# Splitting one weight load and two weight casts into halves, with a newly written order of all steps, in a fused linear-attention and feed-forward kernel

## The chip, the cores and the metric

The kernel runs on one core of one Trainium2 chip. The metric is the device time of one execution in microseconds, the median of several runs. Five engines work side by side, each through its own instruction queue: TensorE (PE in the profile; PEld is its weight load), VectorE (DVE), ScalarE (ACT), GpSimd (POOL) and SyncE (SP), which here issues transfers. An engine takes its instructions strictly in the order in which the program issues them to it, so an instruction that waits holds up all behind it.

## The reference

The first half is a gated linear attention for 4 batches of 8 heads, 768 tokens and a head size of 48: per head a 48x48 state is decayed by a gate and updated for each token, and each output is the query times the state. The second half treats the 3072 tokens with 384 features through a feed-forward layer with h*cos(h) as its nonlinearity.

```python
f = 1.0 / (1.0 + np.exp(-f_logit))
for t in range(S):
    state = f[:, :, t, :, None] * state + np.einsum('bhd,bhe->bhde', k[:, :, t], v[:, :, t])
    y[:, :, t] = np.einsum('bhd,bhde->bhe', q[:, :, t], state)
...
h = x @ w_in            # 3072x384 by 384x2048
g = h * np.cos(h)
return (g @ w_out).astype(np.float32)
```

## The kernel before

**Tiling.** The attention runs over 12 pairs (`pair`, lines 315 to 579), each 256 tokens of one batch for all 8 heads; three pairs make a batch and hand the state on. A pair works in chunk form: gates and their running sums, scaled copies of q and k, scores inside a chunk, sums of k and v over a chunk, and the product with the carried state. The feed-forward layer runs in 13 units (`moe`, lines 589 to 646): units 0 and 1 have 128 tokens each (both halves of pair 0), every later unit m has the 256 tokens of pair m-1. All products are in bf16 with sums in f32. w_in (384x2048) and w_out (2048x384) are loaded as f32 in four quarters each into staging tiles and cast to bf16 (`weights`, lines 275 to 289).

**Steps.** `describe` builds a graph of 930 named steps, each with the engines it may run on and the values it reads and writes. The names used below, with n the pair or m the unit:

- loads on SP (lines 298 to 313): f, k, q, v with n; those of pairs 0 and 1 except v come in two halves by heads (f0.0, f0.1). w0.i and w1.i load quarter i of w_in and w_out (line 286).
- casts of weights: wc0.i and wc1.i (line 288; line 198 in the profile, since `copy` records it).
- ACT: ex, ln, fx, fy make gates from f; eb, ei are exponentials of the running sums; co is the cosine (line 617); xe, ot, vb, vt, sm are copies and casts that several engines may do.
- DVE and POOL: qa, ka (lines 340 to 355) and qm, km (line 408) scale q and k; ad, sd, st, am and g (line 584, the gated product) are elementwise products and sums. zf (line 268), zsp, zqk and zvt are a product of zeros on TensorE that nothing reads, and the clearing of buffers.
- PE: cum (running sums), tq and tk (transpositions; pairs 5 to 11 do them by a DMA), sc (scores), ps (sums over a chunk, line 492), y and yi (outputs, line 545), h (w_in, line 612: `h{m}.{j}{s}` is half s of block j) and o (w_out, line 634: `o{t}.{s}` is quarter s of the sum for token block t).

A unit of 128 tokens reads a whole quarter of w_in in one step h (four blocks of columns, 128 each); a unit of 256 tokens reads half a quarter (two blocks):

```python
G.step(f"h{m}.{j}{s}", ("PE",), first, reads=[xw, w_in_v[(j * F + s * F // 2) // 4]],
       writes=[ph], sums=True)
```

**What sets the order.** Nothing at run time: the text `ORDER` (lines 39 to 118) lists all steps in one sequence, with a letter for the engine (T for PE, S for ACT, V for DVE, G for POOL, Y for SP) and the buffer slots for what the step writes. `emit` (lines 660 to 682) issues them in that order, so each engine's queue is the sequence of its letter, and waits follow from what a step reads, writes and from who had its slot before. The staging tiles of the weights share the slots of g; PSUM is eight banks of 512 (T0 to T7). The 44 zf stand early among the PE steps: TensorE multiplies zeros while the first real inputs come in.

**SP's order before**, as far as it matters: the halves of pairs 0 and 1 with v0, v1 and f2, then w0.0, w0.1, w0.3, w0.2, q2, w1.0, w1.1, k2, w1.2, v2, f3, w1.3, f4, v3, k3, k4, q4, f6, q3.

Of the kernel before, what the change touches and what calls it, by code (L numbers as in the profile page):

```python
# [44 lines left out]
cum1.1:T0 ei1.1:S1 k1.1:Y1 ka0.1:V km0.1:V vb0:G0 vt0.1:G1 qkt0.0:V0 zf23:T3 tk0.1:T k1.0:Y fx1.1:S
v1:Y1 eb1.1:S1 zf24:T3 sc0.0:T4 am0.01:V0 qkt0.1:S1 am0.00:V q1.0:Y f2:Y0 zf25:T3 ps0.0:T0,2 qa1.1:V
vt0.3:S w0.0:Y0 ka1.1:G ex1.0:S ps0.1:T sc0.1:T6 am0.10:V1 sd0.0:V0 am0.11:V st0.1:V km1.1:G1 vt0.2:S
ln1.0:S zf26:T1 zf27:T1 zf28:T1 zf29:T1 zf30:T5 zf31:T5 zf32:T5 cum1.0:T3 vt0.0:S fx1.0:S eb1.0:S
ei1.0:S sm0.0:S0 ka1.0:V vb1:S0 y0.0:T0 zf33:T5 tk1.1:T1 y0.1:T3 w0.1:Y1 vt1.3:S1 vt1.2:S yi0.1:T
xe0.0:S0 km1.0:V qm1.1:V qa1.0:V qm1.0:G zf34:T5 zf35:T5 ps1.1:T6,7 ps1.0:T sd0.1:V0 st1.0:V tq1.1:T  # L50
sd1.0:V1 tk1.0:T4 qkt1.1:V0 w0.3:Y2 w0.2:Y3 sm1.0:G0 zf36:T2 zf37:T2 tq1.0:T zf38:T2 sc1.1:T0 sm0.1:G1
q2:Y0 w1.0:Y4 qkt1.0:V1 ex2:S ln2:S0 xe0.1:S wc0.0:S zf39:T2 sc1.0:T4 zf40:T2 zf41:T2 yi1:T6,2
ad2:G2 zf42:T3 zf43:T3 cum2:T3 vt1.1:G am1.1:V0 vt1.0:G fy2:S h0.00:T0 wc0.1:G am1.0:V1 w1.1:Y0
fx2:S eb2:S0 y1:T st1.1:V xe1.0:V1 ei2:S1 xe1.1:S k2:Y1 sd1.1:V1 h1.00:T4 h2.00:T2 w1.2:Y1
h0.01:T h1.01:T h2.11:T6 wc0.3:G zqk.0:G co0.0:S0 wc0.2:G g0.0:V2 h2.01:T h2.10:T co1.0:S1 g1.0:V
h0.11:T0 co2.1:S2 h0.10:T qa2:G h1.11:T4 h1.10:T co2.0:S0 qm2.1:G0 g2.1:V3 wc1.0:G qm2.0:G co0.1:S1
v2:Y1 co1.1:S2 g2.0:V h2.20:T6 h2.21:T co2.2:S0 h2.31:T2 h2.30:T co2.3:S3 sm1.1:S0 wc1.1:G g0.1:V
g1.1:V g2.2:V o3.0:T0 o0.0:T1 o1.0:T4 tq2.1:T5 o3.1:T tq2.0:T6 o1.1:T f3:Y1 ka2:G km2.1:G
tk2.1:T w1.3:Y4 f4:Y0 v3:Y0 zsp.1:G g2.3:V km2.0:V wc1.2:S ex3:S ln3:S0 fx3:S zqk.2:G
tk2.0:T k3:Y0 vb2:G0 o3.2:T qkt2.1:V0 sc2.1:T2 vt2.1:G0 wc1.3:S vt2.3:G ps2.1:T5 ps2.0:T k4:Y1  # L60
o1.2:T qkt2.0:V1 st2.0:V o0.1:T sc2.0:T6 vt2.0:G q4:Y0 sd2.0:V0 o0.2:T am2.1:V0 sm2.0:G1 yi2:T5,2
ex4:S ln4:S1 vt2.2:G fx4:S ad3:G1 fy4:S ad4:G2 am2.0:V1 y2:T xe2.1:V0 xe2.0:V cum3:T3
o3.3:T o0.3:T ot3:V0 ot0:V1 vb3:G0 o1.3:T h3.20:T6 cum4:T2 eb3:S0 ot1:V2 f6:Y2 ei3:S0
ka3:V km3.0:V0 h3.01:T0 ei4:S1 eb4:S1 h3.00:T h3.21:T km3.1:V ps3.0:T2,3 ps3.1:T ka4:G h3.10:T4
sd3.0:V0 st3.1:V h3.11:T sd3.1:V1 qa4:G h3.31:T2 h3.30:T co3.2:S0 g3.2:V0 o4.2:T6 km4.0:G1 q3:Y1
qm4.0:G qm4.1:G q5:Y2 co3.0:S1 o2.3:T7 f5:Y0 v4:Y0 q6:Y0 sm3.1:S0 co3.1:S2 co3.3:S0 out3:Y
out0:Y g3.0:V tk4.0:T0 g3.1:V km4.1:G fy3:S g3.3:V o4.0:T tk3.0:T1 tq4.1:T4 tq4.0:T qkt4.0:V0
o4.1:T qa3:G vt3.1:G0 tk4.1:T o4.3:T tk3.1:T0 qkt4.1:V1 ex6:S ex5:S ln6:S0 ln5:S1 ot4:S3
qm3.1:V sc4.0:T2 sc4.1:T4 am4.0:V0 o2.2:T tq3.1:T o2.0:T qm3.0:G tq3.0:T o2.1:T f7:Y1 v6:Y1
k6:Y0 k5:Y1 vb4:G1 am4.1:V1 vt4.0:S1 v5:Y0 fx5:S ot2:S0 ad5:G1 o5.0:T2 vt3.3:G qkt3.0:V2  # L70
vt4.3:G ps4.0:T1,3 ps4.1:T sc3.0:T4 qkt3.1:V3 sc3.1:T6 ad6:G2 cum5:T0 o5.2:T vt4.1:S vt4.2:S st4.0:V
sm3.0:G1 vt3.2:G fy6:S fx6:S vt3.0:G o5.3:T sd4.0:V2 cum6:T1 eb5:S0 sm4.0:S2 ei5:S0 am3.0:V2
am3.1:V3 zvt.2:V qa6:G y4:T4,5 yi4:T fy5:S ex7:S eb6:S2 yi3:T0 y3:T6 xe4.1:V0 xe4.0:V
# [116 lines left out]
def describe(nc, cpool, ppool, q, k, v, f_logit, moe_w_in, moe_w_out, out):  # L190
# [72 lines left out]

    if ZEROS:
        for i in range(ZEROS):
            dump = Val(p1)
            dump.bank = i if i < 8 else None
            G.step(f"zf{i}", ("PE",), lambda e, dump=dump: nc.tensor.matmul(  # L268
                dump.ap, lhsT=zero[:, 0:128], rhs=zero, start=True, stop=True), writes=[dump])
# [488 lines left out]
```

## Time and profile before

| what | value |
|---|---|
| median of 3 runs | 178.31 us (178.24 to 178.71) |
| profiled execution | 179.66 us, of which the span from first to last instruction is 177.4 |
| PE busy | 170.8 us (96%), 2470 products |
| DVE, ACT, POOL busy | 136.0, 137.7, 100.1 us |
| clock granted to TensorE | 1.00 throughout |
| read and written in HBM | 25.17 and 4.72 MB |

How to read it: a row of the timeline has start, duration, engine, line, operation, output and inputs, a count, and in brackets how long the engine stood idle before it and what ended that. A row of a transfer is its issue on SP; its landing comes some microseconds later, and the list of transfers gives the time from issue to landing. In the chain of waits a row has start, duration, and the work or wait that the chain went through.

### The profile page before, as it was taken

The numbers are of one execution on the slowest core, as the hardware profiler recorded it, in microseconds if no ns is written. First come the engines' busy times: TensorE is split into PE (matmuls) and PEld (weight loads), VectorE is DVE, ScalarE is ACT, GpSimd is POOL, SyncE is SP. The second block draws the span as 40 slices with busy tenths as digits, with TensorE's granted clock in tenths as the row PEclk, the third lists the DMA queues.
The fourth block names the chain that finished last, engine by engine and source line by source line (L and its number), as shares of the span: only waits on it lengthen the run. The fifth ranks groups of instructions, "written<-read, shape, count | busy, mean of one in ns | idle before, by whom it ended". The sixth has DMA issues, their size and how long they took to land.

```text
span 177.4 us, 5843 instructions
## 1 busy us (share of the span) xinstructions
PE 170.8 (96%) x2470; PEld 124.8 (70%) x2470; DVE 136.0 (77%) x196; ACT 137.7 (78%) x205; POOL 100.1 (56%) x128
## 2 busy tenths in 40 slices
...
DMA  5999999989999975999999999997280030010035
GB/s 127 276 261 306 353 352 351 305 229 280 256 258 286 285 185 134 285 171 235 247 260 279 211 227 232 199 155 163 48 193 2 0 137 4 0 44 4 0 113 198
DMA packets 72281, 33.92 MB, mean 191 GB/s; under 512 B 65344, under 2 KB 70720, under 8 KB 72256
## 3 DMA queue, kind: packets, MB, share of 16 engines
q1 hardware_dynamic: 72256, 33.56, 79.5%
q8 instruction: 19, 0.31, 0.8%
...
HBM read 25.17 MB, written 4.72 MB: 168 GB/s over the span
## 4 chain that ended last, share of the span: by engine, by line
PE 75%; DMA 11%; ACT 3%; DVE 3%; SPq 2%; POOL 2%; issue 1%; DVEq 0%; POOLq 0%
PE ps L634 33%; PE ps L612 28%; DMA g<-in_moe_w_in_dram 5%; DMA v<-in_v_dram 5%; PE ps L545 4%; PE ps L462 3%; SPq L286 2%; PE ps L492 2%; PE ps L268 2%; POOL w_in_bf L198 2%; DMA f<-in_f_logit_dram 2%; PE ps L439 1%; DVE am L474 1%; PE ps L378 1%; DVE qk L408 1%
## 5 line engine op out<-in xcount | busy, mean ns | idle before, releaser
L584 DVE TENSOR_TENSOR g<-ps,co 128x1024 bf16<-128x1024 f32 x48 | 60.1, 1309 | 19.2 <-ACT co L617 16.0
L634 PE MATMUL ps<-w_out_bf,g 128*128 128x384 bf16 (+1 forms) x400 | 69.2, 320 | 0.8 <-ACT w_out_bf L198 0.8
L612 PE MATMUL ps<-x,w_in_bf 128*128 128x256 bf16 (+1 forms) x624 | 66.6, 264 | 0.5 <-POOL w_in_bf L198 0.4
L617 ACT ACTIVATE co<-ps,halfpi 128x1024 bf16<-128x1024 f32 x48 | 51.7, 1113 | 18.2 <-PE ps L612 16.3
L612 PEld LDWEIGHTS <-w_in_bf 128*128 128x128 bf16 x624 | 56.5, 98 | 8.4 <-issue 0.6
L634 PEld LDWEIGHTS <-g 128*128 128x128 bf16 x400 | 37.1, 98 | 21.0 <-issue 1.0
L474 DVE TENSOR_TENSOR am<-ps,pmask 128x1024 bf16<-128x1024 f32 x22 | 26.0, 1216 | 1.5 <-PE ps L462 1.4
L408 POOL TENSOR_TENSOR qk<-q,b 128x384 bf16<-128x384 f32 x18 | 17.8, 1003 | 3.4 <-DVE q L342 2.2
L408 POOL TENSOR_TENSOR qk<-k,bi 128x384 bf16<-128x384 f32 x16 | 16.3, 1027 | 4.8 <-issue 2.0
L198 POOL COPY vt<-vb 64x384 bf16<-64x384 bf16 x31 | 15.3, 503 | 1.4
L268 PE MATMUL ps<-zero 128*128 128x512 bf16 x44 | 13.9, 426 | 1.2 <-DVE zero L204 1.2
L198 ACT COPY ot<-ps 128x384 f32<-128x384 f32 (+1 forms) x13 | 5.9, 450 | 8.9 <-PE ps L634 7.2
L198 POOL CAST vb<-v 128x768 bf16<-128x768 f32 x9 | 7.7, 861 | 8.3 <-DMA v<-in_v_dram 8.3
L333 ACT ACTIVATE f<-f 128x768 f32<-128x768 f32 (+1 forms) x14 | 10.3, 751 | 2.5 <-DMA f<-in_f_logit_dram 2.4
L198 DVE CAST x<-ps 128x384 bf16<-128x384 f32 x16 | 8.4, 550 | 4.5 <-PE ps L545 4.4
L519 POOL TENSOR_TENSOR sz<-sd,half 128x384 bf16<-128x384 bf16 x10 | 8.2, 826 | 5.8 <-DVE sd L509 5.5
L367 POOL TENSOR_TENSOR sp<-ls 128x384 bf16<-128x384 f32 x10 | 10.0, 1001 | 2.6 <-ACT ls L337 2.3
L345 POOL TENSOR_TENSOR q<-f,q 128x384 f32<-128x384 f32 x9 | 9.3, 1037 | 1.0 <-DMA q<-in_q_dram 0.4
L355 POOL TENSOR_TENSOR k<-k,f 128x384 f32<-128x384 f32 (+1 forms) x7 | 6.8, 973 | 4.1 <-DMA k<-in_k_dram 2.0
L198 DVE COPY ot<-ps 128x384 f32<-128x384 f32 (+1 forms) x13 | 6.7, 519 | 3.2 <-PE ps L634 3.0
L462 PE MATMUL ps<-qkt 48*64 48x128 bf16 (+1 forms) x304 | 8.9, 219 | 0.1
L198 ACT COPY vt<-vb 64x384 bf16<-64x384 bf16 x17 | 8.6, 508 | 0.3
...
## 6 DMA issues: line engine op xcount, KB each, us to landing
v<-in_v_dram SPq DMA_DIRECT2D x12, 384.0 KB, 5.8
...
f<-in_f_logit_dram SPq DMA_DIRECT2D x10, 384.0 KB, 6.1
q<-in_q_dram SPq DMA_DIRECT2D x10, 384.0 KB, 5.8
k<-in_k_dram SPq DMA_DIRECT2D x10, 384.0 KB, 6.8
g<-in_moe_w_in_dram SPq DMA_DIRECT2D x4, 768.0 KB, 8.5
g<-in_moe_w_out_dram SPq DMA_DIRECT2D x4, 768.0 KB, 10.7
...
```

The lines of the kernel that those rows point to most:

```text
L198: (nc.scalar.copy if e == "ACT" else eng(e).tensor_copy)(out=o, in_=i)
L268: G.step(f"zf{i}", ("PE",), lambda e, dump=dump: nc.tensor.matmul(dump.ap, lhsT=zero[:, 0:128], rhs=zero, start=True, stop=True), writes=[ ...
L333: nc.scalar.activation(out=flat(t.ap), in_=flat(t.ap), func=AF.Exp, scale=-1.0)
L345: eng(e).tensor_mul(out=w.ap[:, :, 0, :], in0=t.ap[:, :, 1, :], in1=w.ap[:, :, 0, :])
L367: G.step(f"ad{n}", ("POOL",), lambda e: eng(e).tensor_add(out=sp.ap[:, 0, :, 0:D], in0=soft.ap[:, :, 0, :], in1=soft.ap[:, :, 1, :]), read ...
L408: G.step(f"{nm}{n}.{u}", ("POOL", "DVE"), lambda e, u=u, j=j, src=src, dec=dec: eng(e).tensor_mul(out=qkp[u][j].ap[:, :, :, 0:D], in0=swap ...
L462: nc.tensor.matmul(o[t, r, 2 * a + g, :].rearrange("p (e n) -> p e n", e=2), lhsT=w, rhs=qkv(u)[s, 0, a, g, :, :], start=(a == 0 and g == ...
L474: G.step(f"am{n}.{u}", ("DVE",), lambda e, u=u, sc=sc: nc.vector.tensor_mul(out=am[u].ap.rearrange("p r b n -> p (r b) n"), in0=sc.ap.rear ...
L584: nc.vector.tensor_mul(out=o.rearrange("p b (n e) -> p b e n", e=2), in0=ph.ap.rearrange("p (b e n) -> p b e n", e=2, n=64), in1=co.ap.rea ...
L612: nc.tensor.matmul(ph.ap[:, i * T:(i + 1) * T].rearrange("p (g t) -> p g t", t=C), lhsT=w_in_bf[:, kk, f0:f0 + 128], rhs=xa[:, :, kk, :], ...
L617: G.step(f"co{m}.{j}", ("ACT",), lambda e, ph=ph, co=co: nc.scalar.activation(out=co.ap, in_=ph.ap, func=AF.Sin, bias=halfpi), reads=[ph], ...
L634: nc.tensor.matmul(po.ap[:, 0:c1 - c0], lhsT=gap[:, j, i * C:(i + 1) * C], rhs=w_out_bf[:, j, c0:c1], start=(po.first and j == 4 * s), sto ...
```

## The change

Three things change; the amount of real work doesn't.

1. **Halves of w_in.** Quarter 0 is loaded by two transfers (w0.0a, w0.0b, 256 columns each), and quarters 0 and 1 are cast by two steps each (wc0.0a, wc0.0b, wc0.1a, wc0.1b), which DVE may do as well. Steps h of units with 256 tokens then wait for the half they read; those with 128 tokens still read the quarter.
2. **46 zeros** in place of 44, each of the same 512 columns (a width of its own for each can now be given).
3. **A new `ORDER`** of 935 steps, from a planner that also knows where TensorE's instruction blocks end. 88 steps change their engine: vt 21, xe and ot 11 each, sm 8, qm 8, ka 6, and others; out23.0 is issued by ACT in place of SP. PE's order differs in the first third above all: o2.0 to o2.3 now come before ps3, and h3.00 and h3.01 after it.

SP's new order after the halves of pairs 0 and 1, f2, v0 and v1 (the same fifteen loads, with f2 moved ahead of v0): w0.1, w0.0b, w0.0a, w0.3, w0.2, k2, w1.0, q2, w1.1, v2, w1.3, f3, f4, w1.2, f6, v3, k4, k3, q4, q3. ACT's queue has vb1, wc0.1a, sm0.1, vt1.2, xe0.1, wc0.0b in that order; POOL's has wc0.1b, vt1.1, wc0.0a, vt1.3, sm1.0, wc0.3, wc0.2, ka2, km2.1, wc1.0, qa2, qm2.0, km2.0, qm2.1.

```diff
+CUT_LOAD = (0,)
+CUT_CAST = (0, 1)
+SC8 = 1
...
-ZEROS = 44
+ZEROS = (512,) * 46
...
+    w_in_h = [[v.part(lambda a, z=z: a[:, :, 256 * z:256 * z + 256]) for z in range(2)] for v in w_in_v]
...
+        parts = w_in_h[i] if part == 0 and i in CUT_CAST else [dst]
+        n = len(parts)
+        stages = [stage.part(None) for _ in parts] if n > 1 else [stage]
+        if part == 0 and i in CUT_LOAD:
+            for z, st in enumerate(stages):
+                c = slice(256 * z, 256 * z + 256)
+                G.step(f"w{part}.{i}{'ab'[z]}", ("SP",), lambda e, c=c: eng(e).dma_start(
+                    out=view()[:, :, c], in_=src[:, :, c]), writes=[st])
+        else:
+            G.step(f"w{part}.{i}", ("SP",), lambda e: eng(e).dma_start(out=view(), in_=src), writes=[stage])
+        for z, (st, d) in enumerate(zip(stages, parts)):
+            c = slice(w // n * z, w // n * z + w // n)
+            G.step(f"wc{part}.{i}{'ab'[z] if n > 1 else ''}", ("POOL", "ACT", "DVE") if n > 1 else ("POOL", "ACT"),
+                   lambda e, c=c, d=d: copy(e, d.ap, view()[:, :, c]), reads=[st], writes=[d])
...
-                G.step(f"h{m}.{j}{s}", ("PE",), first, reads=[xw, w_in_v[(j * F + s * F // 2) // 4]],
+                G.step(f"h{m}.{j}{s}", ("PE",), first, reads=[xw, w_in_h[j][s] if T == 2 * C and j in CUT_CAST else w_in_v[(j * F + s * F // 2) // 4]],
```

The part of the new order around the first products with w_in, on all engines:

```diff
+zf44:T6 ps1.0:T vt1.1:G tq1.0:T2 tk1.0:T wc0.0a:G vt1.3:G st1.0:V w1.1:Y0 qkt1.0:V0 h0.01:T6
+sd1.0:V1 xe0.1:S h1.01:T4 wc0.0b:S fx2:S v2:Y1 vt1.0:S sm1.0:G1 sc1.0:T0 wc0.3:G am1.0:V1 st1.1:V
+sd1.1:V0 wc0.2:G h1.00:T h0.00:T yi1:T0,1 y1:T co1.0:S0 zf45:T2 h1.11:T2 xe1.1:V1 xe1.0:S co0.0:S1
```

More of the change, by code (lines that the diff above doesn't have):

```diff
@@ L45 @@
[L45 to L73, printed above, removed]
@@ L113 @@
[L113 to L117 removed]
+zqk.2:V f0.1:Y0 f0.0:Y ex0.0:S zqk.0:G zsp.2:G ex0.1:S ln0.1:S2 ln0.0:S q0.1:Y0 fx0.1:S qa0.1:V
@@ new lines @@
+qkt0.0:V1 w0.1:Y0 am0.10:V0 am0.11:V zf26:T2 zf27:T2 zf28:T2 zf29:T2 sc0.0:T6 am0.01:V1 w0.0b:Y1 ad2:G2
+w0.0a:Y w0.3:Y2 w0.2:Y3 vt0.3:S0 fx1.0:S eb1.1:S1 zf30:T0 zf31:T0 zf32:T0 ps0.0:T2,0 ps0.1:T cum2:T4
+k2:Y0 qa1.1:V ka1.1:V w1.0:Y4 am0.00:V eb2:S2 vt0.0:S ei1.0:S zf33:T5 zf34:T5 zf35:T5 zf36:T5
+zf37:T1 zf38:T1 y0.0:T5 qm1.1:G0 sd0.0:V0 st0.1:V vt0.2:G qa1.0:V km1.1:V sm0.0:G0 eb1.0:S vt0.1:S
+zf39:T6 zf40:T6 zf41:T6 y0.1:T1 ei2:S1 xe0.0:S0 ka1.0:G tq1.1:T3 tk1.1:T vb1:S0 q2:Y0 sd0.1:V1
+qkt1.1:V2 wc0.1a:S zf42:T6 zf43:T6 yi0.1:T sc1.1:T4 ps1.1:T0,3 sm0.1:S0 km1.0:V vt1.2:S0 qm1.0:V am1.1:V0
@@ new lines @@
+wc0.1b:G zf44:T6 ps1.0:T vt1.1:G tq1.0:T2 tk1.0:T wc0.0a:G vt1.3:G st1.0:V w1.1:Y0 qkt1.0:V0 h0.01:T6
+sd1.0:V1 xe0.1:S h1.01:T4 wc0.0b:S fx2:S v2:Y1 vt1.0:S sm1.0:G1 sc1.0:T0 wc0.3:G am1.0:V1 st1.1:V
+sd1.1:V0 wc0.2:G h1.00:T h0.00:T yi1:T0,1 y1:T co1.0:S0 zf45:T2 h1.11:T2 xe1.1:V1 xe1.0:S co0.0:S1
+h2.01:T0 h2.00:T g1.0:V2 h1.10:T fy2:S w1.3:Y1 ka2:G km2.1:G0 wc1.0:G qa2:G f3:Y1 co2.0:S0
+sm1.1:S0 qm2.0:G km2.0:G g0.0:V f4:Y0 co1.1:S1 h2.31:T4 h0.10:T6 h2.30:T qm2.1:G g2.0:V3 h0.11:T
+co2.3:S0 g1.1:V w1.2:Y4 co0.1:S2 h2.11:T0 h2.10:T h2.21:T2 h2.20:T g2.3:V o0.0:T4 o1.0:T5 f6:Y2
@@ new lines @@
+co2.1:S1 g0.1:V g2.1:V v3:Y0 tk2.0:T6 tq2.0:T k4:Y0 k3:Y1 q4:Y0 tq2.1:T7 tk2.1:T qkt2.0:V0
+vb2:G0 vt2.3:G0 wc1.1:S co2.2:S0 o2.0:T0 o1.1:T qkt2.1:S1 g2.2:V sc2.1:T6 ps2.0:T1 ps2.1:T wc1.3:G
+vt2.1:G st2.0:V sd2.0:V1 sm2.0:V1 vt2.2:G ex3:S sc2.0:T2 am2.0:V0 ln3:S0 fx3:S ad3:G0 am2.1:V1
+vt2.0:G o2.1:T o3.0:T1 o0.1:T o3.3:T o3.1:T ex4:S o0.3:T yi2:T2,3 fy3:S y2:T ln4:S0
+cum3:T6 o2.3:T fy4:S wc1.2:G o3.2:T o2.2:T ad4:G0 cum4:T7 o0.2:T vb3:G0 eb3:S0 fx4:S
+ex6:S ln6:S0 fx6:S vt3.3:G0 q3:Y1 xe2.1:V0 xe2.0:V ot2:V0 ot3:V1 ka4:G ot0:V2 eb4:S1
@@ new lines @@
+ei4:S0 h3.20:T2 o1.2:T ei3:S1 h3.21:T v4:Y0 ka3:V km3.1:V0 k5:Y2 km3.0:V h3.10:T0 o1.3:T
+ps3.1:T4,6 qa4:V ps3.0:T sd3.0:V0 km4.1:G2 km4.0:G co3.2:S0 h3.11:T f5:Y0 q6:Y2 out0:Y qm4.1:G
+ot1:S3 qa3:G h3.01:T4 h3.00:T fy6:S g3.2:V0 h3.30:T2 h3.31:T co3.1:S1 qm4.0:G g3.1:V f7:Y1
+co3.0:S0 vt3.0:S tq4.1:T7 o4.1:T0 qm3.0:G co3.3:S1 tk4.1:T g3.0:V v5:Y1 out3:Y vt3.1:G o4.2:T
+tk3.0:T1 st3.1:V g3.3:V tk4.0:T4 o4.0:T sd3.1:V1 tq4.0:T qkt4.0:V0 qkt4.1:S1 tq3.0:T o4.3:T vb4:S1
+qm3.1:G vt4.0:G2 ad6:G0 ps4.1:T2,3 ps4.0:T q5:Y0 k7:Y0 k6:Y1 qkt3.0:V2 st4.0:V sd4.0:V2 ex5:S
@@ L118 @@
+o22.3:T o20.0:T ot22.0:S1 o23.3b:T0 ot22.1:S out22.0:Y out22.1:Y g11.2:V o21.2:T o20.2:T ot20:S2 o18.1:T
+ot18:S1 o21.0:T out20:Y out18:Y ot21:V3 out21:Y o23.2b:T o23.0b:T o23.1b:T ot23.1:S out23.1:Y
 """
```

124 lines of the change are left out of this document (60 added, 64 removed).

## The prediction

> **What bounds the kernel now.** I read the page first, then busy time by stage, then the timeline of single engines in the stages where TensorE loses time, then the transfers.
>
> ```profile
> span 177.4 us, 5843 instructions
> PE 170.8 (96%) x2470; PEld 124.8 (70%) x2470; DVE 136.0 (77%) x196; ACT 137.7 (78%) x205; POOL 100.1 (56%) x128
> DMA  5999999989999975999999999997280030010035
> ```
>
> TensorE is busy 96% of the span, and the transfers (third row, slices of 4.4 us) are full for the first third. The table by stage has span, then busy time of PE, PEld, DVE, ACT and POOL, clock, DMA share and GB/s.
>
> ```profile
> 1.00:21.30 20.30, 19.53 (x269) 10.31 (x269) 16.08 (x48) 16.70 (x36) 8.56 (x15) 1.00 1.08 273
> 21.30:33.10 11.80, 11.38 (x176) 10.49 (x177) 7.69 (x9) 10.66 (x13) 9.27 (x9) 1.00 1.09 352
> 33.10:49.50 16.40, 15.22 (x204) 9.81 (x202) 13.81 (x18) 13.72 (x20) 12.19 (x16) 1.00 1.04 258
> 49.50:174.30 124.80, 124.69 (x1823) 94.19 (x1823) 98.31 (x124) 96.08 (x138) 69.71 (x85) 1.00 0.72 157
> ```
>
> From 49.5 us to the last product TensorE idles 0.1 us in 124.8. So the end is fixed by two numbers: when TensorE enters this gapless stretch, and how much work it has left then. Only the stages before can be won. They lose 1.18 us in 33.10:49.50 and 0.42 us in the stage ahead; the first stage is partly filled with products of zeros, so its busy time hides waiting.
>
> ```profile
> 27.86 5.46 PE L612 MATMUL ps<-x,w_in_bf 128*128 128x128 bf16 x72 [0.39 <-POOL w_in_bf L198]
> 38.71 0.81 PE L634 MATMUL ps<-w_out_bf,g 128*128 128x384 bf16 x4 [0.83 <-ACT w_out_bf L198]
> 49.57 0.31 PE L492 MATMUL ps<-vb,qk 64*64 64x48 bf16 x16 [0.17 <-DVE qk L408]
> ```
>
> All three waits end with a chain from a load: a quarter of w_in, a quarter of w_out, and (third row, step ps3.1) the k tile of pair 3. The rows of a chain below show how.
>
> **The zeros and the tail.**
>
> ```profile
> 5.83 2.53 PE L268 MATMUL ps<-zero 128*128 128x512 bf16 x11
> 167.10 7.19 PE ps L634 x56
> 174.31 0.32 ACT ot L198
> 50.54 0.37 SPq L300 DMA_DIRECT2D f<-in_f_logit_dram  x1
> ```
>
> Eleven zeros span 2.53 us with a last one of 0.38, so one takes (2.53 - 0.38) / 10 = 0.215 us, and two more 0.43 us. I cost them at nothing: they stand before h1.11, where TensorE will wait for weights anyway (next part). If that cover were gone they would cost 0.43 us. The tail stays: after the last product ot23.1 takes 0.32 us on ACT and its store follows. The one store that moves is out23.0, from SP's queue to ACT's. No row shows a transfer issued by ACT; an issue takes 0.37 us on SP (third row), so it costs at most that on ACT ahead of ot23.1, and gains at most that on SP ahead of out23.1: -0.4 to +0.4. I take 0, since both queues have some microseconds between out23.0 and the last step.
>
> **The first products with w_in.**
>
> ```profile
> 12.33 1.44 SPq L286
> g<-in_moe_w_in_dram SPq DMA_DIRECT2D x1, 768.0 KB, 7.2
> 24.26 1.47 POOL L198 CAST w_in_bf<-g 128x1536 bf16<-128x1536 f32 x1 [0.80 <-DMA g<-in_moe_w_in_dram]
> 26.38 1.47 POOL L198 CAST w_in_bf<-g 128x1536 bf16<-128x1536 f32 x1 [0.18 <-DMA g<-in_moe_w_in_dram]
> 15.52 0.82 ACT L198 CAST vb<-v 128x768 bf16<-128x768 f32 x1
> 14.83 0.79 ACT L517 ACTIVATE sz<-sd,mine 128x192 bf16<-128x192 bf16 x2
> 11.69 0.51 ACT L198 COPY vt<-vb 64x384 bf16<-64x384 bf16 x1
> 17.32 0.47 ACT L198 CAST x<-ps 128x384 bf16<-128x384 f32 x1
> ```
>
> The first quarter of w_in is issued at 12.33 us and lands 7.2 us later, at 19.5. In both plans the same fifteen loads stand ahead of the w_in quarters, so in the new plan quarter 1, now first, lands at 19.5 and both halves of quarter 0 by 21.9. A half cast moves 128x768, like vb: 0.82 us in place of 1.47. That splits a wait: the first half could be cast 1.1 us sooner. But units 0 and 1 (128 tokens) still read the whole quarter; only unit 2 reads halves, and it comes later in both plans. So the halves bring nothing on TensorE's path. Splitting the load into rows of 1 KB costs between 0 (rows of 1.5 and 2 KB move alike) and 0.7 us (the difference from twice a 384 KB tile at the pace below, 2.9 us, to 2.2); I take 0, the nearer rows.
>
> The half cast wc0.1a puts a wait into ACT's queue: ACT stands until 19.5 us for quarter 1, and sm0.1, vt1.2 and xe0.1 queue behind. h1.01 needs xe0.1: 19.5 + 0.82 + 0.79 + 0.51 + 0.47 = 22.1 us, and I put TensorE there about 0.5 us earlier. This is hidden by the next wait; without that it would cost the 0.5. Quarters 3 and 2 land where they land now, since the same bytes are ahead: POOL's casts end at 24.26 + 1.47 = 25.7 and 26.38 + 1.47 = 27.85 us. h1.10 reads quarter 2, so it can't start before 27.87, just as h0.11 today (27.86). Up to the first product with w_out both plans have done the same set (but for the two zeros). Today that product, o3.0, starts at 33.15; in the new plan nine steps h of 0.66 us stand from h1.10 to o0.0, which so comes at 27.87 + 5.94 = 33.8. TensorE is 0.65 us behind here.
>
> The Trainium skill, in "DMA: Bandwidth & Descriptors", section "Rules for kernel authors", says that splitting a transfer into two partition halves isn't worth it because both use the same 16 engines in turn. Here the cut is by columns; no run shown has it, and by that rule the term would be 0 too, with no gain from the earlier half.
>
> **The second pair of loads: POOL's queue.**
>
> ```profile
> 31.14 1.46 POOL L198 CAST w_out_bf<-g 128x1536 bf16<-128x1536 f32 x1 [1.16 <-DMA g<-in_moe_w_out_dram]
> 28.98 1.01 POOL L408 TENSOR_TENSOR qk<-q,b 128x384 bf16<-128x384 f32 x1
> 8.36 0.22 PE ps L439 x4
> 39.45 0.40 PE L462 MATMUL ps<-qkt 48*128 48x128 bf16 x8
> 40.14 1.48 PE L634 MATMUL ps<-w_out_bf,g 128*128 128x384 bf16 x8
> 42.63 0.52 PE L545 MATMUL ps<-qkt,sz 128*32 128x128 bf16 x24
> 44.16 2.11 PE L634 MATMUL ps<-w_out_bf,g 128*128 128x384 bf16 x12
> ```
>
> Today q2 lands ahead of w_out's first quarter, and POOL has qa2 and one qm2 done when that quarter lands at 31.1. The new SP order is k2, w1.0, q2: w1.0 again at about 31.1, for the same bytes are ahead, and q2 1.45 us later (the pace is worked out below). POOL's order is ka2, km2.1, wc1.0, qa2, qm2.0, km2.0, qm2.1: 31.14 + 1.46 + 4 x 1.01 = 36.65 us. The transposition tq2.1 waits for that; TensorE would reach it at 33.8 + 1.3 (o0.0, o1.0) + 0.45 (two transpositions of 0.22) = 35.55. So it loses 1.1 us there, about what this whole stage loses today (1.18). From tq2.1 to ps3.0 the plan has 14 steps o and 3 steps h (9.1 + 2.0 by the prices below), and scores, sums, transpositions and two cum for 3.2 (today 0.69 from 39.45 to 40.14 and 1.5 from 42.63 to 44.16; the other scores, cum4 and the transpositions make up the rest): 14.3 us, so ps3.0 at 50.95.
>
> **The k tile of pair 3.** This is the term that decides.
>
> ```profile
> 38.70 2.77 SPq L300 DMA_DIRECT2D k<-in_k_dram  x1
> k<-in_k_dram SPq DMA_DIRECT2D x1, 384.0 KB, 7.7
> 46.12 1.57 SPq L300 DMA_DIRECT2D q<-in_q_dram  x1
> q<-in_q_dram SPq DMA_DIRECT2D x1, 384.0 KB, 6.1
> 46.79 0.79 DVE L355 TENSOR_TENSOR k<-k,f 128x384 f32<-128x384 f32 x1
> 47.69 1.83 DVE L408 TENSOR_TENSOR qk<-k,bi 128x384 bf16<-128x384 f32 x2
> ```
>
> Today k3 is issued at 38.70 and lands 7.7 us later at 46.4; four tiles on, q3 lands at 46.12 + 6.1 = 52.2. So the full queue passes a 384 KB tile each (52.2 - 46.4) / 4 = 1.45 us. The new SP order puts everything ahead of k3 that is ahead of it today, and f6 and k4 as well: 46.4 + 2 x 1.45 = 49.3 us. Behind it stands the same chain, all on DVE: ka3, km3.1, km3.0, and the product. Today it takes from 46.79 to 49.57, 2.78 us. In the new plan: 49.35 + 2.78 = 52.1 us for ps3.0, later than the 50.95 at which TensorE would be there. ps3.0 is 2.55 us later than ps3.1 today.
>
> What is left then:
>
> ```profile
> 91.33 10.48 PE ps L612 x96
> 76.59 3.90 PE ps L634 x24
> ```
>
> Six products with w_in (a step h) take 0.655 us, four with w_out (a step o) 0.65. At ps3.0 the new plan has done h3.10 and o2.0 to o2.3, which today come after ps3.1, and still owes h3.00 and h3.01, which come before: 0.655 + 4 x 0.65 - 2 x 0.655 = 1.95 us less to do. 2.55 - 1.95 = +0.6 us.
>
> **The gapless stretch.** Steps, engines and shapes are the same; 88 steps change engine, mostly vt, xe, ot, ka in both directions. I cost it at the same 0.1 us of idle time. What covers it is slack of DVE (98.3 of 124.8) and ACT (96.1); POOL has 69.7.
>
> **Sum.** Against the profiled execution: last product from 174.3 to 174.9, span 178.0 in place of 177.4. That execution took 179.66 us, 2.3 over its span and 1.35 over the median of the runs shown (178.31). The difference carries over: 178.31 + 0.6 = **178.9 us**. About 0.3% (0.53 us) is what a measurement of this kernel can tell from no change, so this lies at the edge of it.
>
> **Rivals.**
>
> 1. *Faster: the queue of loads stops lagging.* Between the landings at about 26.3 and 31.1 us only q2 and w1.0 pass, worth 1.45 + 2.12 (26.38 - 24.26) = 3.6 us, but 4.8 went by: 1.2 us were lost.
>
> ```profile
> q1 hardware_dynamic: 72256, 33.56, 79.5%
> q8 instruction: 19, 0.31, 0.8%
> ```
>
> The page's second queue carries 19 blocks of instructions over the run, on the same engines. If a plan that knows where these blocks fall keeps them off the loads, w1.0 and k3 come 1.2 us sooner: tq2.1 at 35.6, ps3.0 at 50.9, and 50.9 - 49.57 - 1.95 = -0.6 us; with a small gap elsewhere filled, -0.8: 177.5 us. For it: the 1.2 us exist. Against it: about as many instructions have been issued by then in either plan, so the block falls at about the same time. It decides if k3 lands before 48.7. The Trainium skill, in "Runtime: NRT & Kernel Launch", section "Instruction fetch mechanics", says that instructions come in blocks of 16 KiB and that crossing one is mostly hidden; 0.31 MB in 19 agrees with the size, and by that rule this rival would be worth 0.
>
> 2. *Slower still: POOL falls behind in the first gapless microseconds.* POOL's qm4.1 waits for qa4, which DVE does behind km3.0: about 52.8 us. Then POOL has qm4.1, qa3, qm4.0, qm3.0, qm3.1, ad6, ad5 at 1.0 us each, five vt at 0.5 and sm4.0 at 0.8: ad5 ends at about 63.1. cum5 needs it, some 12.6 us of products after ps3.0: 64.7. If POOL loses 2.6 us on that way, cum5 waits 1.0 us: 179.9. It decides if qm4.1 starts after 54.4. For it: POOL waits for loads (q3, v4) twice on that way. Against it: the later TensorE comes, the wider the margin.
>
> 3. *Nothing:* the start only moves its waits, k3 comes some 0.5 us sooner than the full queue allows today: 178.3.
>
> **Chances.** The forecast 0.42 (178.4 to 179.4, 0.25 of it beyond 0.3%), rival 1 0.28 (0.25 beyond), rival 2 0.17, rival 3 0.13. Faster 0.25; same 0.17 + 0.03 + 0.13 = 0.33; slower 0.25 + 0.17 = 0.42. The range takes in rival 1 and rival 2 with half of the tail's bound on either side: 177.3 to 180.1.
>
> **What would show it.** k3 landing at about 49.3 us and ps3.0 at about 52; tq2.1 waiting about 1 us for POOL near 36; the first wait of TensorE for w_in ending at about 27.9; no more than 0.2 us idle after that. Wrong would be: k3 before 48.7, a TensorE that enters the gapless stretch without a wait for DVE, or idle time of over 0.5 us after 55 us.

## The result and the profile after

The changed kernel takes 180.47 us (median of 4 runs, 180.26 to 181.14) where the kernel before took 178.51 beside it: a ratio of 1.0117, with a 95% interval of 1.0085 to 1.0150. It is 2.0 us slower. The prediction said 178.9 (177.3 to 180.1): slower as forecast, but by more than three times as much. The profiled execution took 180.34 us, its span 178.6.

The page of the changed kernel, in the same rows as before (its line numbers are 11 higher in the steps, so 612 is now 623, 634 is 645, 408 is 419, 492 is 503, 617 is 628; `copy` is 201, the loads 311):

```profile
span 178.6 us, 5860 instructions
PE 171.1 (96%) x2472; PEld 125.0 (70%) x2472; DVE 134.4 (75%) x190; ACT 136.7 (77%) x203; POOL 105.9 (59%) x134
DMA  5999999999999995999957999185939503010024
```

TensorE has 0.3 us more to do, the span is 1.2 us longer than the one on which the prediction was built. That is too little for 2.0 us, so the base has to be looked at too. The kernel before was profiled once more (run e0_before below: 178.37 us, span 176.2). First the stages of that execution, cut at the first product with w_in, the first with w_out, the second half of ps3 and the start of the last product; then the changed kernel cut at the same four events. Columns as in the prediction: span, busy time of PE, PEld, DVE, ACT and POOL, clock, DMA share, GB/s.

```profile
1.00:21.43 20.43, 19.61 (x270) 10.34 (x270) 16.10 (x48) 16.71 (x36) 8.58 (x15) 1.00 1.10 284
21.43:33.24 11.81, 11.43 (x176) 10.53 (x177) 7.71 (x9) 10.68 (x13) 10.78 (x10) 1.00 1.10 345
33.24:48.33 15.09, 14.78 (x205) 9.84 (x203) 12.94 (x18) 13.68 (x20) 10.73 (x15) 1.00 1.16 266
48.33:172.76 124.43, 124.41 (x1823) 94.14 (x1823) 98.91 (x123) 95.90 (x138) 70.10 (x85) 1.00 0.68 157
```

```profile
1.00:20.90 19.90, 19.10 (x239) 9.70 (x239) 13.64 (x42) 14.65 (x33) 9.95 (x16) 1.00 1.05 264
20.90:34.23 13.33, 12.56 (x211) 11.34 (x210) 10.75 (x14) 13.12 (x20) 11.70 (x12) 1.00 1.11 344
34.23:51.36 17.13, 16.32 (x215) 10.83 (x213) 12.98 (x18) 16.31 (x24) 14.05 (x16) 1.00 1.18 279
51.36:175.05 123.69, 122.89 (x1812) 93.11 (x1813) 96.91 (x119) 92.00 (x129) 69.78 (x86) 1.00 0.69 152
```

Read the last rows first. The kernel before enters its gapless stretch at 48.33 us in this execution, not at 49.57, and idles 0.02 us in it. The changed kernel enters at 51.36, 3.03 us later, and idles 0.80 us in a stretch that the prediction costed at 0.1. The stretch is 124.43 - 123.69 = 0.74 us shorter; without its wait of 0.9 us (below) it would be some 1.65 shorter, where the prediction had 1.95 less work. The sum is 3.03 - 0.74 = 2.29 us at the last product. The rows above show where the later entry comes from. 0.9 us of the 3.03 are idle time: span less PE's busy time grew from 0.38 to 0.77 us in the second row and from 0.31 to 0.81 in the third, and stayed at 0.8 in the first. The other 2.2 us are busy time: steps that the new order does ahead of ps3, and the two zeros.

The runs are 2.0 us apart and the spans 2.4, because less time lies outside the span after the change: 1.74 us in the profiled execution (180.34 less 178.6), 2.17 before (178.37 less 176.2). The run with the halves alone, below, shows with which part of the change this comes.

TensorE's waits over the whole changed execution (what waited, for what, us in total, times, longest), and the three products behind them on the timeline:

```profile
PE ps L623 <- ACT x L201: 1.5, 2, 0.8
PE ps L503 <- DVE qk L419: 0.8, 1, 0.8
```

```profile
22.50 0.83 PE L623 MATMUL ps<-x,w_in_bf 128*128 128x128 bf16 x12 [0.77 <-ACT x L201]
51.36 0.31 PE L503 MATMUL ps<-vb,qk 64*64 64x48 bf16 x16 [0.81 <-DVE qk L419]
131.29 1.47 PE L623 MATMUL ps<-x,w_in_bf 128*128 128x256 bf16 x12 [0.76 <-ACT x L201]
```

These are h1.01 (waits for xe0.1), ps3.0 (for km3.0) and h10.30 (for xe9.1). From issue to issue they cost 0.93, 0.99 and 0.92 us above the usual step. Each has its own cause.

**h10.30.** ACT in the changed kernel around it:

```profile
126.42 0.50 ACT L410 ACTIVATE b<-ps 128x392 f32<-128x392 f32 x1
128.46 1.28 ACT L628 ACT_TABLE_LOAD   x1 [1.54 <-issue]
129.75 1.11 ACT L628 ACTIVATE co<-ps,halfpi 128x1024 bf16<-128x1024 f32 x1
130.77 0.47 ACT L201 CAST x<-ps 128x384 bf16<-128x384 f32 x1
```

xe9.1 (130.77) was moved from DVE to ACT and stands behind co9.0. That cosine needs another function table than the exponentials before it, and the load of the table is issued only once co9.0's own wait (for h9.01) is over: ACT stands idle for 1.54 us and then spends 1.28 us on the load.

**ps3.0.** Three chains end together: k3's load (issue on SP, then the time to landing), the exponential ei3 on ACT (behind ex6, ln6, fx6, eb4 and ei4), and the copies ot2, ot3, ot0, which stand ahead of ka3 on DVE:

```profile
42.15 1.28 SPq L311 DMA_DIRECT2D k<-in_k_dram  x1
k<-in_k_dram SPq DMA_DIRECT2D x1, 384.0 KB, 6.0
```

```profile
46.17 1.49 DVE L201 COPY ot<-ps 128x384 f32<-128x384 f32 x3 [1.28 <-PE ps L645]
47.61 0.86 ACT L410 ACTIVATE bi<-ps 128x384 f32<-128x384 f32 x2
48.20 0.56 DVE L366 TENSOR_TENSOR k<-k,f 128x384 f32<-128x384 f32 x1 [0.55 <-ACT bi L410]
48.23 2.65 POOL L419 TENSOR_TENSOR qk<-k,bi 128x384 bf16<-128x384 f32 x2 [0.17 <-ACT bi L410]
48.90 2.41 DVE L419 TENSOR_TENSOR qk<-k,bi 128x384 bf16<-128x384 f32 x2
```

The copies end at 47.66 us, k3 lands at 48.12, ei3 ends at 48.47. k3 was the last that ka3 waited for. An estimate from these rows: with k3 there sooner, ka3 could follow the copies and km3 start with the end of ei3, near 48.5 in place of 48.90, some 0.4 us of the 0.99; either of the other two moved alone would win nothing. The last two rows show a fourth thing: km3 on DVE and km4 on POOL run side by side and slow each other (2.41 us for two, 2.65 for two).

**h1.01.** As the prediction described it, ACT stands until quarter 1 is there, and xe0.1 is cast behind:

```profile
20.01 0.83 ACT L201 CAST w_in_bf<-g 128x768 bf16<-128x768 f32 x1 [1.55 <-DMA g<-in_moe_w_in_dram]
21.99 0.47 ACT L201 CAST x<-ps 128x384 bf16<-128x384 f32 x1
```

### The profile page after: what moved, and what is told of

Read it like the earlier page. It is cut to its first block, busy times and chain, and to the rows that moved or that the text cites. A ratio compares the mean times of both kernels' runs of the same rounds, so it can differ in the third digit from the quotient of the medians.

```text
span 178.6 us, 5860 instructions
## 1 busy us (share of the span) xinstructions
PE 171.1 (96%) x2472; PEld 125.0 (70%) x2472; DVE 134.4 (75%) x190; ACT 136.7 (77%) x203; POOL 105.9 (59%) x134
## 4 chain that ended last, share of the span: by engine, by line
PE 69%; DMA 8%; ACT 8%; SPq 6%; issue 4%; DVE 2%; POOL 1%; DVEq 0%; ACTq 0%; POOLq 0%
PE ps L623 30%; PE ps L645 28%; SPq L311 6%; DMA g<-in_moe_w_in_dram 4%; PE ps L556 4%; DMA q<-in_q_dram 4%; ACT co L628 3%; PE ps L473 3%; PE ps L503 2%; DVE am L485 1%; PE ps L450 1%; ACT sz L528 1%; PE ps L389 1%; ACT L688 1%; POOL w_out_bf L201 1%
## 5 line engine op out<-in xcount | busy, mean ns | idle before, releaser
L623 PE MATMUL ps<-x,w_in_bf 128*128 128x256 bf16 (+1 forms) x624 | 67.4, 264 | 1.5 <-ACT x L201 1.5
L419 POOL TENSOR_TENSOR qk<-q,b 128x384 bf16<-128x384 f32 x18 | 18.4, 1029 | 7.3 <-DVE q L356 2.7
L419 POOL TENSOR_TENSOR qk<-k,bi 128x384 bf16<-128x384 f32 x17 | 17.6, 1042 | 3.3 <-issue 2.9
L366 POOL TENSOR_TENSOR k<-k,f 128x384 f32<-128x384 f32 (+1 forms) x11 | 10.5, 953 | 5.0 <-ACT b L406 4.2
L201 DVE COPY ot<-ps 128x384 f32<-128x384 f32 x12 | 6.5, 553 | 5.4 <-PE ps L645 5.1
L530 POOL TENSOR_TENSOR sz<-sd,half 128x384 bf16<-128x384 bf16 x11 | 9.1, 827 | 0.6 <-DVE sd L520 0.3
L201 DVE CAST x<-ps 128x384 bf16<-128x384 f32 x13 | 6.9, 553 | 3.2 <-PE ps L556 3.0
L628 ACT ACT_TABLE_LOAD x6 | 7.7, 1283 | 1.6 <-issue 1.5
L270 PEld LDWEIGHTS <-zero 128*128 128x128 bf16 x46 | 4.4, 107 | 6.1 <-issue 2.2
```

The costliest lines, as they stand in the source:

```text
L201: (nc.scalar.copy if e == "ACT" else eng(e).tensor_copy)(out=o, in_=i)
L270: G.step(f"zf{i}", ("PE",), lambda e, dump=dump, w=w: nc.tensor.matmul(dump.ap[:, 0:w], lhsT=zero[:, 0:128], rhs=zero[:, 0:w], start=True, ...
L366: eng(e).tensor_mul(out=w.ap[:, :, 0, :], in0=w.ap[:, :, 0, :], in1=t.ap[:, :, 0, :])
L419: G.step(f"{nm}{n}.{u}", ("POOL", "DVE"), lambda e, u=u, j=j, src=src, dec=dec: eng(e).tensor_mul(out=qkp[u][j].ap[:, :, :, 0:D], in0=swap ...
L623: nc.tensor.matmul(ph.ap[:, i * T:(i + 1) * T].rearrange("p (g t) -> p g t", t=C), lhsT=w_in_bf[:, kk, f0:f0 + 128], rhs=xa[:, :, kk, :], ...
L628: G.step(f"co{m}.{j}", ("ACT",), lambda e, ph=ph, co=co: nc.scalar.activation(out=co.ap, in_=ph.ap, func=AF.Sin, bias=halfpi), reads=[ph], ...
```

## The experiments

The diffs of the order show of each line only the steps around those that move.

**The kernel before, once more.**

> The kernel before once more, profiled on the chip that runs the experiments. It settles how its span belongs to its time: the profile of before had a span of 177.4 us in an execution of 179.66, while the median of its runs is 178.5. If the profiled execution was a long one, span and time here are both about 1 us lower (span near 176.5, last product near 173.3); if the 1 us lies outside the span, the span is again 177.4.

178.52 us (10 runs), ratio 0.9992 (0.9976 to 1.0008). Its trace is the base used above. In the execution on which the prediction rests w_out's first quarter landed at 17.08 + 14.0 = 31.1 us; here the timeline of SP has its issue, and the list of transfers the time to landing:

```profile
17.01 5.24 SPq L286 DMA_DIRECT2D g<-in_moe_w_out_dram  x1
```

```profile
g<-in_moe_w_out_dram SPq DMA_DIRECT2D x1, 768.0 KB, 12.5
```

That is 29.5 us, 3.5 us behind the last quarter of w_in (25.9), which is the pace that the prediction worked out (3.6). In the changed kernel and in the kernel with the halves alone it landed at 29.9. So the 1.2 us that the queue had lost belong to that one execution and not to the order; what caused them there is not known. The step o3.2, for which TensorE waited 0.83 us there (38.71 in the prediction's rows), starts at 37.50 here with hardly a wait (0.1 us).

**xe9.1 back on DVE.**

```diff
-xe9.0:V0 g9.0:V qm11.1:V xe9.1:S
+xe9.0:V0 xe9.1:V g9.0:V qm11.1:V
```

> The new kernel with xe9.1 on DVE right behind xe9.0, not on ACT behind co9.0. Theory A (TensorE pays for steps that stand in a queue behind another wait): h10.30 no longer waits for ACT, the idle 0.92 us at 131.3 us shrinks to under 0.1, and the time falls by 0.8 to 0.9 us to about 179.6. Theory B (the engines are too full after 51 us, and a wait that is taken away comes back at the next step): the idle time moves to another step within 10 us and the time falls by under 0.3.

180.89 us, ratio 1.0119 (1.0093 to 1.0144): no gain. h10.30 no longer waits, but the next step that hangs on the late cosine does. In its timeline g9.0 waits for co9.0, and o17.0 for g9.0:

```profile
131.38 1.31 DVE L595 TENSOR_TENSOR g<-ps,co 128x1024 bf16<-128x1024 f32 x1 [1.03 <-ACT co L628]
132.75 0.82 PE L645 MATMUL ps<-w_out_bf,g 128*128 128x384 bf16 x4 [0.43 <-DVE g L595]
```

So moving xe9.1 was not the cause by itself. That it is the table load behind the wait is shown by the run with the load ahead, below.

**k3's load alone ahead.**

```diff
-g2.3:V o0.0:T4 o1.0:T5 f6:Y2
+g2.3:V o0.0:T4 o1.0:T5 k3:Y1 f6:Y2
-tq2.0:T k4:Y0 k3:Y1 q4:Y0
+tq2.0:T k4:Y0 q4:Y0
```

> The new kernel with the load k3 ahead of f6, v3 and k4. Theory A: k3 lands about 2.9 us sooner (two tiles of 1.45), near 45.3 us, DVE's chain to ps3.0 ends by 50, the idle 0.99 us ahead of ps3.0 goes, and the time falls by 0.9 to 1.0 us to about 179.5. Theory B: f6, v3 or k4, 1.45 us later each, take the place (ka4 and km4.1 on POOL, then tq4.1), and the time falls by under 0.3.

181.02 us, ratio 1.0125 (1.0098 to 1.0152). k3 landed at 44.1 us, 4 us sooner, and ps3.0 still came at 51.61. The execution profiled is a long one, though (181.76 us): TensorE waits 0.42 us for a cast of w_in at 21.56 and is 0.66 us late at h1.11 (26.84, where the changed kernel has 26.18), ahead of anything that the edit moves. Counted from there ps3.0 comes some 0.4 us sooner, and its wait is 0.40 us in place of 0.81. What is left of it is ei3, the second of the two exponentials below: it ends at 49.13, and km3 starts there.

```profile
48.27 0.86 ACT L410 ACTIVATE bi<-ps 128x384 f32<-128x384 f32 x2
49.22 2.33 DVE L419 TENSOR_TENSOR qk<-k,bi 128x384 bf16<-128x384 f32 x2 [0.22 <-ACT bi L410]
```

The load that the prediction called the deciding term is only one of three chains, and the 0.4 us don't show in the time: 1.0125 here, 1.0117 for the changed kernel, each known to some 0.3%.

**xe0.1 ahead of the half cast.**

```diff
-qkt1.1:V2 wc0.1a:S zf42:T6 zf43:T6 yi0.1:T sc1.1:T4
+qkt1.1:V2 zf42:T6 zf43:T6 yi0.1:T xe0.1:S wc0.1a:S sc1.1:T4
-sd1.0:V1 xe0.1:S h1.01:T4
+sd1.0:V1 h1.01:T4
```

> The new kernel with xe0.1 ahead of wc0.1a in ACT's queue, so that it doesn't stand behind the wait for w_in's quarter 1. Theory A: the idle 0.93 us ahead of h1.01 goes, but only about 0.4 us of it reaches the first product with w_out (quarter 2's cast ends at 27.8 whatever is done), and nothing of that reaches the end, since ps3.0 waits for k3: 180.4, within 0.2 of the new kernel. A rival: the 0.93 us at h1.01 is what makes the kernel slower; then the time falls by 0.8 to 0.9 us to about 179.6.

180.63 us, ratio 1.0113 (1.0080 to 1.0147): h1.01's wait is gone, and the time is the same within the 0.3% of either interval. TensorE waits 0.45 us at h1.00 and 0.32 at h1.11 for weights, and for ps3 as long as ever. "Hidden by the next wait" was right for this one.

**All three chains at ps3.0.**

```diff
-g2.3:V o0.0:T4 o1.0:T5 f6:Y2
+g2.3:V o0.0:T4 o1.0:T5 k3:Y1 f6:Y2
-eb3:S0 fx4:S
+eb3:S0 ei3:S1 fx4:S
-xe2.0:V ot2:V0 ot3:V1 ka4:G ot0:V2 eb4:S1
+xe2.0:V ka3:V km3.1:V0 km3.0:V ot2:V0 ot3:V1 ka4:G ot0:V2 eb4:S1
```

> The changed kernel with the three chains that end at ps3.0 all moved forward: k3's load ahead of f6's, ei3 directly behind eb3 on ACT (ahead of ex6, ln6, fx6), and ka3, km3.1, km3.0 on DVE ahead of the copies ot2, ot3, ot0. Theory A (the loss lies in three separate places, and a wait that is removed whole stays removed): ps3.0's 0.99 us is gone, the stretch behind it starts some 0.9 us sooner, 179.5 us, ratio to the kernel before 1.005 to 1.007. Theory B (the order behind is just as full, so that each wait comes back at the next step): the stretch starts sooner, but waits of 0.5 us and more appear among h3.11 to h3.31 or y4, and the time stays at 180.2 to 180.6.

180.13 us, ratio 1.0075 (1.0048 to 1.0102), so some 0.7 us of the 2.0 are back. In its trace DVE does ka3 and km3 some three and two microseconds sooner, and both halves of ps3 follow without a wait, at 50.69 us:

```profile
45.13 1.25 DVE L366 TENSOR_TENSOR k<-k,f 128x384 f32<-128x384 f32 x1
46.52 1.78 DVE L419 TENSOR_TENSOR qk<-k,bi 128x384 bf16<-128x384 f32 x2
48.23 1.47 DVE L201 COPY ot<-ps 128x384 f32<-128x384 f32 x3
50.69 0.44 PE L503 MATMUL ps<-vb,qk 64*64 64x48 bf16 x32
```

h10.30 waits 0.92 us as before. k3 moved alone gave nothing in the time, the three chains together did; neither of the other two was moved alone. The time lies between the theories (A 179.5, B from 180.2), the ratio just over A's.

**The table load ahead of the wait.**

```diff
         n0 = nc.next_id()
         s.fn(e)
...
         apart(tc, users, s, e, [i for i in made if i is not None])
+        if s.name == "eb11":
+            nc.scalar.preload_act_table_set("trig_and_small")
```

> The changed kernel with one instruction more: the function table of the sine is asked for directly behind eb11, the last exponential on ACT, instead of just ahead of co9.0, where it waits for h9.01. Nothing else moves, and xe9.1 stays on ACT. Theory A: the 1.28 us table load runs in the 1.5 us in which ACT stands idle, co9.0 starts when h9.01 ends, xe9.1 is written 1.28 us sooner, h10.30's wait of 0.92 us is gone and nothing takes its place: 179.5 us, ratio 1.005 to 1.007. Theory B: the 0.9 us comes back at o17.0 or sc10.1, as when xe9.1 was moved to DVE: 180.2 to 180.6.

180.07 us, ratio 1.0071 (1.0047 to 1.0094): about 0.8 us back, and nothing came in its place. ACT, and the stretch behind ps3.0, in its trace:

```profile
127.59 1.28 ACT L695 ACT_TABLE_LOAD   x1
129.13 1.11 ACT L628 ACTIVATE co<-ps,halfpi 128x1024 bf16<-128x1024 f32 x1 [0.26 <-issue]
130.14 0.47 ACT L201 CAST x<-ps 128x384 bf16<-128x384 f32 x1
```

```profile
52.00:175.04 123.04, 123.02 (x1813) 93.14 (x1813) 97.12 (x119) 91.67 (x128) 70.01 (x86) 1.00 0.70 153
```

The load now runs in the idle time of ACT. With xe9.1 still on ACT, TensorE idles 0.02 us in the stretch, as in the kernel before.

**All three waits together.** The two edits above and xe0.1 ahead.

> The two edits of the runs beside it together, and xe0.1 ahead of the cast of the first half as well, so that all three waits are addressed. Theory A: the two gains add, and the 0.93 us at h1.01, which the wait at ps3.0 had absorbed, shows too: 178.2 to 178.8, at the kernel before or a little under it. Theory B: 179.5 or more.

179.43 us, ratio 1.0032 (1.0009 to 1.0055), between the two theories. The gains add, 0.42% and 0.46% to 0.85%. Each gain by itself stands at the edge of its intervals; the sum is clear of them (1.0085 to 1.0150 for the changed kernel). Some 0.6 us over the kernel before remain in the time; in the span it is twice that (177.75 us on average, 176.56 before), because less lies outside it. In this trace, of an execution 0.7 us longer than the median, TensorE waited for weights in the opening (1.4 us over three steps) and for transposes:

```profile
PE ps L623 <- POOL w_in_bf L201: 0.9, 2, 0.5
PE ps L473 <- DMA qkt<-qk: 0.7, 2, 0.5
PE ps L623 <- ACT w_in_bf L201: 0.5, 1, 0.5
```

**Two transposes ahead on SP**, on top of that.

```diff
-ei9:S0 k10:Y1 out9:Y tq8.1:Y3
+ei9:S0 tq8.1:Y3 k10:Y1 out9:Y
-out6:Y tq11.1:Y2 out10:Y tq10.1:Y0 out14:Y
+out6:Y tq11.1:Y2 tq10.1:Y0 out10:Y out14:Y
```

> The kernel with all three waits addressed, and two transposes moved forward on SP: tq8.1 ahead of k10's load and out9, tq10.1 ahead of out10. In the trace without this edit TensorE waited 0.4 us at sc7.1, 0.6 us at sc8.1 and 0.35 us at sc10.1 for transposes. Theory A (what is left over the kernel before are further single places of this kind): sc8.1's and sc10.1's waits are gone, ratio 0.998 to 1.001. Theory B (the order is full, every earlier start is taken up by the next wait): 1.002 to 1.004, as without the edit.

179.77 us, ratio 1.0044 (1.0017 to 1.0071): not better than without, though its trace has no wait for a transpose left. The twelve executions lie between 178.45 and 181.74 us, so a gain of some 0.2% can't be ruled out; a cure of all that remains can.

**The halves alone**, in the kernel before and its order.

```diff
-vt0.3:S w0.0:Y0
+vt0.3:S w0.0a:Y0 w0.0b:Y
-xe0.1:S wc0.0:S
+xe0.1:S wc0.0a:S wc0.0b:S
-h0.00:T0 wc0.1:G
+h0.00:T0 wc0.1a:G wc0.1b:G
```

> The kernel before with the halves alone: the first quarter of w_in is loaded as two halves and the first two quarters are cast as two halves each, every half in the place and on the engine where the whole stood; order, zeros and all else as before. The prediction put this part at nothing (0 to 0.7 for the split load): 178.5, ratio 0.998 to 1.002. If the halves themselves cost something (a DMA more on the load queue, two casts more on ACT and POOL), 178.9 to 179.3.

178.46 us, ratio 0.9975 (0.9960 to 0.9990). The split load and the split casts cost nothing, and all of the loss is the new order. The 0.25% that they win isn't on TensorE's path: the spans average 176.6 us, as those of the kernel before beside it. What falls is the time outside the span, from 2.2 us to 1.8, and it is 1.7 to 1.9 us in every execution of every kernel that has the halves. Here out23.0 is still issued by SP, so its move to ACT isn't the reason; which part of the code is, stays open. Against this kernel, which has about the same time outside its span as the changed one, the new order costs 1.3% (1.0108 over 0.9975), or 2.4 us, and with all three waits addressed 0.6%, or 1.0 us. This is also the fastest kernel of the study.

**Two zeros fewer** (zf44 and zf45 taken out of the changed kernel).

> The changed kernel without zf44 and zf45, so with the 44 multiplications by zeros that the kernel before has. The prediction put the two at nothing, because h1.11 behind them waits for weights anyway: ratio as that of the changed kernel, 1.010 to 1.014. If they lie on the path, 0.2 to 0.43 us less: 1.008 to 1.010.

180.39 us, ratio 1.0096 (1.0075 to 1.0118), beside 1.0108 for the changed kernel measured with it (next): no difference that can be told, where the intervals are as wide as the 0.24% that two zeros could cost. In place of the zeros TensorE waited 0.4 us ahead of ps1.0 and 0.5 us ahead of tq1.0.

**The changed kernel again**, as the base of the last four runs.

> The changed kernel once more, unaltered, with more executions than its first measurement, as the base for the others: ratio to the kernel before 1.010 to 1.014. Where the three places named so far carry the loss (theory A), its trace shows h1.01, ps3.0 and h10.30 waiting again, each by 0.7 to 1.2 us; if it is chance (theory B), the waits stand in other places in this execution.

180.43 us, ratio 1.0108 (1.0077 to 1.0138). The same three places wait: h1.01 0.65 us, ps3.1 and ps3.0 0.73 and 0.34, h10.30 0.92. They belong to the order, not to one execution.

**The cure of ps3 in the kernel before**, with the halves.

```diff
-am2.0:V1 y2:T xe2.1:V0 xe2.0:V cum3:T3
-o3.3:T o0.3:T ot3:V0 ot0:V1
+am2.0:V1 o3.3:T y2:T xe2.1:V0 xe2.0:V cum3:T3 eb3:S0 ei3:S0
+o0.3:T ka3:V km3.0:V0 km3.1:V ot3:V0 ot0:V1
```

> The kernel before with the halves, and around ps3 the cure that the changed kernel showed: o3.3 goes ahead of y2 to cover y2's wait of 0.35 us for DVE, eb3 and ei3 stand right behind cum3 on ACT, and ka3, km3.0, km3.1 stand ahead of the copies ot3, ot0, ot1 on DVE, so that they run beside less of POOL's work. Theory A (a wait removed whole stays removed): y2's 0.35 and ps3.1's 0.32 us are gone, ratio 0.993 to 0.996. Theory B (the copies now free the PSUM banks later, and h3.01 or h3.21 waits instead): 0.997 to 1.002.

182.36 us, ratio 1.0173 (1.0131 to 1.0215), far worse than either theory said. o3.3 now waits 0.93 us for its weights, and the copies behind km3 free the PSUM banks of h3.01 too late. First the place in the kernel with the halves alone, then here, each from its own timeline, and the clock here by windows:

```profile
45.90 2.12 PE L623 MATMUL ps<-x,w_in_bf 128*128 128x256 bf16 x18
```

```profile
48.87 3.79 PE L623 MATMUL ps<-x,w_in_bf 128*128 128x256 bf16 x18 [2.21 <-DVE ot L201]
```

```profile
44.00:46.60 2.60, 2.60 (x32) 1.00 1.07 255
48.87:52.60 3.73, 3.73 (x21) 0.54 0.95 214
```

The wait of 2.2 us was paid nearly twice: behind it the granted clock was 0.54 for 3.7 us, and the same 18 products took 3.79 us in place of 2.12. The six executions agree: in four the mean clock of the span was 0.99 and they took 182.28 to 183.70 us, in the other two it was 1.00 and they took 180.63 and 180.87. So the lower clock goes with some 1.7 us more, and the executions without it still lie 2 us over the kernel before.

## Why the prediction was wrong, step by step

- *The halves and the split load at nothing:* right for TensorE's path (the same span; 0.9975 in the time, from outside the span). The Trainium skill, in "DMA: Bandwidth & Descriptors", section "Rules for kernel authors", says of two transfers to partition halves that they aren't worth it; the prediction carried that over to a cut by columns, and the run agrees.
- *The two zeros at nothing:* nothing was seen, and 0.43 us is at the edge of what the run could tell.
- *The tail at nothing, with 0.4 us either way:* 0.4 us less lies outside the span after the change. The same is seen in the kernel with the halves alone, so it isn't out23.0's engine.
- *h1.01 0.5 us late, hidden by the next wait:* 0.93 us, and hidden; taking it away alone changed nothing. h1.10 came at 28.29 (27.87 forecast), o0.0 at 34.23 (33.8).
- *tq2.1 1.1 us late for POOL:* it came at 35.98 us without a wait. w1.0 landed at 29.9, not at 31.1, because the 1.2 us lag wasn't a property of the order. From there to ps3 TensorE took 14.26 us, as forecast (14.3).
- *Rival 1:* its mechanism fell with that. The kernel before lands w1.0 at 29.5 in an ordinary execution, so there was nothing to win; its sign, k3 before 48.7, came true (48.12), and the time rose all the same. The profiles of both executions have the same 19 blocks of instructions, and the lag is in one and not in the other, so the blocks alone don't make it. That agrees with the rule of the Trainium skill ("Runtime: NRT & Kernel Launch", section "Instruction fetch mechanics") that crossing from one block to the next is mostly hidden.
- *Rivals 2 and 3:* cum5 doesn't wait, and the difference is clear of the noise.
- *k3 at 49.3 us and ps3.0 at 52.1, the deciding term:* k3 landed at 48.12, ps3.0 came at 51.36. The place was right, but the load was not what decided it in the kernel before. There k3 landed at 46.41, and DVE went from the copies ot3, ot0, ot1 to ka3 (46.79) without a pause: ka3 waited for the copies. First the copies in the execution of the prediction; then k3 (issue and time to landing), the copies and ka3 in the ordinary one, where k3 had landed 0.6 us before ka3 began:

```profile
45.01 1.86 DVE L198 COPY ot<-ps 128x384 f32<-128x384 f32 x3
```

```profile
37.87 2.35 SPq L300 DMA_DIRECT2D k<-in_k_dram  x1
k<-in_k_dram SPq DMA_DIRECT2D x1, 384.0 KB, 7.1
43.81 1.86 DVE L198 COPY ot<-ps 128x384 f32<-128x384 f32 x3
45.58 0.75 DVE L355 TENSOR_TENSOR k<-k,f 128x384 f32<-128x384 f32 x1
```

In the changed kernel k3 was the last, but by less than 0.5 us: the prediction's sum had neither ei3 nor the copies. And the chain from ka3 to ps3.0 took 3.16 us in place of 2.78, with km3 at 2.41 us beside km4 on POOL (1.83 before).
- *1.95 us less work behind ps3.0:* some 1.65, by either of the two stretches: the changed kernel's less its wait, or the one of 123.04 us without a wait, of which 0.25 are the last product itself, against 124.43. Where the other 0.3 went was not traced.
- *"The difference carries over"* is the first term of the sum that failed. The prediction took the 1.35 us by which its profiled execution lay over the median to be the same for both kernels. In the kernel before, 1.24 of it lay ahead of ps3.1 (49.57 there, 48.33 in an ordinary execution). In the changed kernel ps3.0 came only 0.74 us sooner than forecast from that execution (51.36, not 52.1). So the delay didn't cancel, and the entry into the stretch is 3.03 us later, not 2.55.
- *The gapless stretch at 0.1 us of idle time* is the second, and the largest. "Slack of DVE and ACT" was read as an average, though 88 steps had changed engines. One of them, xe9.1, landed behind a table load: 0.92 us. The prediction's list of what would make it wrong had this ("idle time of over 0.5 us after 55 us"), but no step of its working went through the moved steps one by one.

The sum with the measured terms: 3.03 - 1.65 + 0.9 = 2.3 us at the last product, where the prediction had 2.55 - 1.95 + 0 = 0.6. Of the 1.7 us that it lacked, 0.9 are the idle stretch, 0.5 the entry and 0.3 the work. The median differs by 2.0 and not by 2.3 because 0.4 us less lies outside the span. That the change came out slower, as forecast, is in part luck: the wait that was to decide it has another make-up, and the largest term was put at nothing.

Shown by runs: the halves cost nothing; the waits at ps3.0 and h10.30 are worth 0.7 and 0.8 us, and they add. Not settled: the last 1.0 us, measured against the kernel with the halves alone (0.6 against the kernel before). The opening is the likeliest place. TensorE reaches h2.01 at 26.99 us where the kernel before does at 26.10, and has one step h (0.65 us) less done by then; at the first product with w_out, with the same steps done but for the zeros, it is 0.99 us behind (34.23, 33.24). But no experiment isolates it.
